# The last transform stage of one batch inside the loop, and loads asked for in another order, in a spectral layer with a gated feed-forward on one core

## Chip, cores and metric

The kernel runs on one core of a Trainium2 chip. The metric is the device time of one execution in microseconds (us). Before the change its median is 1721.03 us over three runs (1718.88 to 1724.48).

## What is computed

```python
X = np.fft.rfft(x, axis=1)                      # x: 8 batches x 3136 x 256
Yr = Xr @ w_r - Xi @ w_i + b_r
Yi = Xr @ w_i + Xi @ w_r + b_i
Yr = np.sign(Yr) * np.maximum(np.abs(Yr) - 0.01, 0.0)     # and Yi alike
y = np.fft.irfft(Y, n=3136, axis=1)
h = np.maximum(y @ w_in, 0.0)                   # 256 -> 1024
conv_out = sum(conv_w[k] * hp[:, k:k + S, :] for k in range(3))
out = (h * (1.0 / (1.0 + np.exp(-conv_out)))) @ w_out     # 1024 -> 256
```

The three feed-forward weights come as float64 and are turned into pairs of float32 values (a high and a low part) on the chip.

## The kernel before

The program has two halves. The first, the transform loop, does the Fourier transform, the complex weights, the shrinking and the first half of the inverse transform. The second, the feed-forward loop, finishes the inverse transform (stage 4) batch by batch and runs the two large matrix products.

**Transform loop.** The work is 56 items, seven per batch (`items`, line 385). An item goes through stage 1 (`stage1_pe`, `stage1_out`, line 272: load 224 KB x 2 of x, multiply, copy the result `a1` out of PSUM by ACT and DVE, store it to a scratch tensor `sc1`), stage 2 (`stage2`, line 313, which reads the scratch back as `a2`), `third` (ACT, then POOL writes `fl`), `mix` (line 341, three PSUM banks of 12 matmuls each, then DVE adds into `p1` and `v`), `shrink` (two ACT Relu into `r` and `q`, then POOL subtracts) and `stage3_pe`/`stage3_out` (line 364 and 370, result `z1` stored to the scratch `sc2`). The items are pipelined: in pass `it` of the loop PE does stage 3 of item `it-4`, stage 1 of an item some eight ahead, stage 2 of item `it` and the mix of item `it-1`. The whole half stands under `manual_schedule`, so each engine executes in the order in which the code is written. Stage 1 reads ahead by three loads of x (`fetch(XRB)`), a2 is asked for one or two passes ahead, except at a batch's first item, which is asked for one pass ahead.

**The head.** Ahead of the loop, `stage1_head` does stage 1 of batch 0's seven items. Half of each x load and all of the `ha` stores are issued by ACT, the rest by SP. Between the x loads and the first a2 load SP also asks for the first mixing weights (`load_mix`), two pieces of the table t2, and four more x loads (`fetch(2)`).

**Weights.** From pass 7 on, a generator `later()` is advanced three steps a pass (lines 432 to 439). Each step is one DVE instruction of the float64 conversion; the DMA that brings a piece (`load_bits`, line 201) is one of its steps, asked for while the piece before it is converted. The table i2 and the convolution weights `cw` are asked for after the last piece.

**Between the halves.** Stage 4 (`stage4`, lines 473 to 495) reads back 448 KB of `sc2` as `z2`, does 8 matmuls (line 482; the trace shows 16 records, as each fp32 matmul goes in two passes) into two PSUM banks, and moves them to `yh` (ACT, line 488) and `yl` (DVE, line 489), two or three strided pieces each, ACT and DVE in turn. A batch takes seven calls. Batch 0's seven stand ahead of the feed-forward loop, after the transform's last pass, since the memory for y (two tiles of 25 KB a partition) is free only then. Here, and in the whole second half, a scheduler orders the instructions.

**Feed-forward loop.** 224 steps of `up` (12 matmuls, line 507, then ReLU, the three-tap convolution, sigmoid and gating on ACT and DVE) and, four steps later, `down` (21 matmuls, line 535). Stage 4 of the next batch is put in at f = 1, 4, 7.

All DMA commands of one engine are issued in program order, and a command that waits holds those behind it. A command also waits until the one eight places before it, whose completion counter it takes over, is done.

Of the kernel before, what the change touches and what calls it, by code (L numbers as in the profile page):

```python
# [18 lines left out]
R = 56  # L19
U = 28  # L20
SL = 57
SP = 64
# [8 lines left out]
CH = 448  # L31

# [92 lines left out]
def spectral_ffn_kernel(ctx: ExitStack, tc: tile.TileContext, x, w_r, w_i, b_r, b_i,  # L125
# [18 lines left out]

    with ExitStack() as ab:
        stg = ab.enter_context(tc.tile_pool(name="stg", bufs=1))
        wbp = ab.enter_context(tc.tile_pool(name="wbp", bufs=2))
        s1p = ab.enter_context(tc.tile_pool(name="s1p", bufs=2))
# [7 lines left out]
        f1 = c1.tile([P, P], F32, name="f1")[:, 0:SP]  # L156
# [41 lines left out]
        def load_bits(src, n, name):  # L198

            raw = wbp.tile([P, n, 2], I32, name=f"{name}_bits", tag="bits")  # L200
            nc.sync.dma_start(raw.rearrange("p (a b) w -> p a b w", a=src.shape[1]) if len(src.shape) == 4 else raw, src)
            return raw
# [33 lines left out]
        def later():  # L236
# [7 lines left out]
            for n in range(len(pieces) + 1):  # L244
                if n < len(pieces):
                    dst, src, nm = pieces[n]
                    asked.append((dst, load_bits(src, WP, nm), WP, nm))
                    yield None
                if n:
                    yield from split_weight(*asked.pop(0))  # L250
            nc.sync.dma_start(i2, inv2.rearrange("p (a m) -> p a m", a=2))
            bits = [load_bits(conv_w[k].rearrange("(f p) w -> p f w", p=P), NF, "cw") for k in range(2)]
            for k in range(3):
                top, rest = yield from from_bits(bits[k], NF, "cw")
                yield nc.vector.tensor_tensor(cw[:, k, :], top, rest, op=ALU.add)
                if k == 0:
                    bits.append(load_bits(conv_w[2].rearrange("(f p) w -> p f w", p=P), NF, "cw"))

        def load_x(pool, b, jc, q=nc.sync, **kw):
# [3 lines left out]
            for h in range(2):  # L263
                (q if h else nc.sync).dma_start(xr[SP * h:SP * h + R], xv[h, :, jc * JC:(jc + 1) * JC, :])
# [9 lines left out]
        def store_a1(b, jc, a1, q=nc.sync):  # L274
            dst = sc1[b].rearrange("m (c r j) d -> r c m (j d)", r=2, j=4)
            for r in range(2):
                q.dma_start(dst[r, jc], a1[SP * r:SP * r + R].rearrange("p j h d -> p (j h d)"))  # L277
# [14 lines left out]

        def stage1_head(xs):

            with tc.tile_pool(name="ha", bufs=1, reuse_waits="tile") as ha:
                for jc, xr in enumerate(xs):
                    a1 = ha.tile([P, 2, 2, D], F32, name=f"ha{jc}")
                    copy_a1(a1, stage1_pe(xr))
                    store_a1(0, jc, a1, nc.scalar)
# [28 lines left out]
        def mix(xs):  # L328
# [13 lines left out]
            p1 = wk.tile([K2, 2, UG // 2, D], F32, name="p1")  # L342
            v = wk.tile([K2, 2, UG // 2, D], F32, name="v")
            for c in range(2):
                nc.vector.tensor_tensor(p1[:, c], ps[2], bias[:, c:c + 1, :].to_broadcast([K2, UG // 2, D]), op=ALU.add)
            for c in range(2):
                nc.vector.tensor_tensor(v[:, c], ps[c], p1[:, c], op=ALU.add)
            return v

        def shrink(v):  # L350
            r = wk.tile([K2, 2, UG // 2, D], F32, name="r", bufs=3)
            q = wk.tile([K2, 2, UG // 2, D], F32, name="q", bufs=1)
            nc.scalar.activation(r, v, AF.Relu, bias=mlam)
            nc.scalar.activation(q, v, AF.Relu, bias=mlam, scale=-1.0)  # L354
            nc.gpsimd.tensor_tensor(r, r, q, op=ALU.subtract)  # L355
# [43 lines left out]
        with tc.tile_pool(name="hx", bufs=1, reuse_waits="tile") as hx:  # L399
            xh = [load_x(hx, 0, p, nc.scalar, tag=f"hx{p}") for p in range(NG)]  # L400
            load_t2(0)
            raw = load_mix()
            fetch(2)
            load_t2(1)
            stage1_head(xh)
            split_mix(raw)
            a2s = {i: load_a2(*items[i]) for i in range(2)}
# [7 lines left out]
        background = later()  # L415
        for it in range(n_it + LAG):
# [15 lines left out]
            if WP0 <= it < n_it:  # L432
                next(background, None)
# [166 lines left out]
```

## Time and profile before

| | |
|---|---|
| median of three runs | 1721.03 us |
| the profiled execution's own time | 1719.61 us |
| its span in the trace | 1717.8 us, so 1.8 us lie around it |
| PE busy | 1676.3 us |
| DVE, ACT, POOL busy | 1390.6, 1197.7, 209.9 us |
| granted PE clock over the span | 0.989 |
| mean share of the DMA engines busy in the first 430 us | 0.7 to 0.9 and over |

Rows of the view of waits read: engine, tile and line that waited, what ended the wait, total us, times, longest. Rows of the chain and of the timeline read: start, duration, engine, line, operation, tile written and read; in the timeline the bracket gives the engine's idle time just before it and what ended it. Rows of the windows give the stretch, then each engine's busy us with its count, the granted PE clock, the mean share of the 16 DMA engines, GB/s. Consecutive PE records overlap by some tenths of a us, so prices are taken from start to start.

### The profile page before, as it was taken

To read this page: it belongs to the slowest core of one execution; us is meant where nothing else is said; L and a number is where in the kernel's file an instruction comes from. 1 tells how busy PE (TensorE), PEld (TensorE's weight loads), DVE (VectorE), ACT (ScalarE), POOL (GpSimd) and SP (SyncE) were. 2 spreads that over 40 slices of the span, in tenths; PEclk is the share of its full clock that TensorE was granted. 3 is DMA by queue.
4 is the path that set the end of the run, shared out by engine and by line. 5 is a ranking of instruction groups with operands and counts; after the bars stand their busy time and mean duration, and the time that the engine had idled before them with its cause. 6 is when DMAs were issued, how large, how long until landed. Compare 5 with 4: busy or idle time off the path is not lost.

```text
span 1717.8 us, 30462 instructions
## 1 busy us (share of the span) xinstructions
PE 1676.3 (98%) x12544; PEld 1553.5 (90%) x12544; DVE 1390.6 (81%) x1722; ACT 1197.7 (70%) x1589; POOL 209.9 (12%) x116
## 2 busy tenths in 40 slices
PE   4999999999989999999999999999999999999998
PEld 1888888888878999999999999999999999999998
DVE  2678888776547888888888888888888888888887
ACT  2667777767656777777777777777777777777676
POOL 0344544444520000000000000000000000000000
PEclk7999999999999999999999999999999999999999
DMA  8998888788441110111111011111101111100001
GB/s 242 265 268 256 238 248 246 222 233 219 122 126 34 55 43 22 54 55 33 54 45 43 22 55 52 35 55 44 43 22 55 48 39 47 40 22 23 22 22 44
DMA packets 109002, 163.77 MB, mean 95 GB/s; under 512 B 10680, under 2 KB 87728, under 8 KB 108864
## 3 DMA queue, kind: packets, MB, share of 16 engines
q1 hardware_dynamic: 107394, 157.01, 31.4%
q10 hardware_dynamic: 1470, 4.82, 0.8%
q8 instruction: 99, 1.62, 0.4%
q14 instruction: 39, 0.32, 0.1%
HBM read 84.73 MB, written 77.07 MB: 94 GB/s over the span
## 4 chain that ended last, share of the span: by engine, by line
PE 96%; DMA 2%; ACT 1%; DVE 1%; issue 0%; ACTq 0%; POOL 0%; SPq 0%
PE acc L535 32%; PE ps_h L507 32%; PE ps_mx L341 14%; PE ps_s L313 7%; PE ps_s L482 6%; PE ps_s L364 3%; PE ps_s L272 3%; DMA xr<-in_x_dram 1%; DMA sc<-ha 0%; DVE yl L489 0%; DMA sc<-a 0%; ACTq L277 0%; DMA sc<-z 0%; DVE c L516 0%; ACT yh L488 0%
## 5 line engine op out<-in xcount | busy, mean ns | idle before, releaser
L535 PE MATMUL acc<-wout,gh 128*128 128x256 f32 x3136 | 571.2, 281 | 0.0
L516 DVE SCALAR_TENSOR_TENSOR c<-h,cw,c 128x896 f32<-128x896 f32 x448 | 512.0, 1146 | 69.7 <-ACT c L514 66.7
L507 PE MATMUL ps_h<-yh,win 128*128 128x450 f32 x1792 | 550.1, 368 | 3.0 <-ACT yh L488 2.0
L535 PEld LDWEIGHTS acc<-wout,gh 128*128 128x128 f32 x3136 | 493.0, 188 | 6.1 <-ACT gh L521 0.2
L535 PE MATMUL acc<-wout,gl 128*128 128x256 f32 x1568 | 437.3, 280 | 0.4 <-DVE gl L522 0.4
L507 PEld LDWEIGHTS ps_h<-yh,win 128*128 128x128 f32 x1792 | 339.5, 189 | 29.3 <-ACT yh L488 2.2
L509 ACT ACTIVATE h<-ps_h 128x900 f32<-128x900 f32 x224 | 207.0, 924 | 197.8 <-PE ps_h L507 197.4
L507 PE MATMUL ps_h<-yl,win 128*128 128x450 f32 x896 | 329.9, 368 | 0.2 <-DVE yl L489 0.2
L535 PEld LDWEIGHTS acc<-wout,gl 128*128 128x128 f32 x1568 | 293.8, 188 | 1.2 <-DVE gl L522 0.6
L518 DVE TENSOR_TENSOR c<-h,c 128x896 f32<-128x896 f32 x224 | 243.2, 1086 | 40.9 <-ACT c L517 40.1
L522 DVE TENSOR_TENSOR gl<-c,gh 128x896 fp32r<-128x896 f32 x224 | 242.5, 1088 | 41.7 <-ACT gh L521 40.8
L521 ACT CAST gh<-c 128x896 fp32r<-128x896 f32 x224 | 210.7, 941 | 85.7 <-DVE c L518 85.7
L517 ACT ACTIVATE c<-c 128x896 f32<-128x896 f32 x224 | 212.4, 948 | 20.3 <-DVE c L516 18.3
L341 PE MATMUL ps_mx<-wmix_hi,fh 128*128 128x256 f32 x672 | 192.6, 287 | 0.0
L341 PE MATMUL ps_mx<-wmix_hi,fl 128*128 128x256 f32 x672 | 188.3, 280 | 1.7 <-POOL fl L325 1.7
L341 PE MATMUL ps_mx<-wmix_lo,fh 128*128 128x256 f32 x672 | 187.5, 279 | 0.0
L507 PEld LDWEIGHTS ps_h<-yl,win 128*128 128x128 f32 x896 | 169.5, 189 | 11.6 <-DVE yl L489 0.5
L514 ACT ACTIVATE c<-h,cw 128x896 f32<-128x896 f32 x168 | 176.0, 1047 | 1.8
L355 POOL TENSOR_TENSOR r<-r,q 128x1024 f32<-128x1024 f32 x56 | 133.4, 2382 | 236.8 <-ACT q L354 229.3
L313 PEld LDWEIGHTS ps_s<-t,a 112*128 112x128 f32 x896 | 106.0, 194 | 54.4 <-issue 47.9
L341 PEld LDWEIGHTS ps_mx<-wmix_hi,fl 128*128 128x128 f32 x672 | 126.3, 188 | 2.5 <-POOL fl L325 1.9
L313 PE MATMUL ps_s<-t,a 112*128 112x128 f32 x896 | 117.0, 284 | 10.9 <-issue 10.2
(75 smaller groups left out, 1713.3 us busy)
## 6 DMA issues: line engine op xcount, KB each, us to landing
a<-sc SPq DMA_DIRECT2D x56, 448.0 KB
z<-sc SPq DMA_DIRECT2D x56, 448.0 KB
out_dram<-o SPq DMA_DIRECT2D x27, 896.0 KB
xr<-in_x_dram SPq DMA_DIRECT2D x105, 224.0 KB
sc<-z SPq DMA_DIRECT2D x104, 224.0 KB
sc<-a SPq DMA_DIRECT2D x98, 224.0 KB
sc<-ha ACTq DMA_DIRECT2D x14, 224.0 KB
win_bits<-in_moe_w_in_dram SPq DMA_DIRECT2D x4, 512.0 KB
```

Source lines behind the costliest of these rows:

```text
L313: nc.tensor.matmul(ps[:, k], a2[:, k, t * P:(t + 1) * P], t2[:, g * UG + k, :], start=(k == 0), stop=(k == UG - 1), skip_group_check=True)
L341: nc.tensor.matmul(ps[c][:, k, :], lt, rh, start=(n == 0), stop=(n == len(mm) - 1))
L355: nc.gpsimd.tensor_tensor(r, r, q, op=ALU.subtract)
L507: nc.tensor.matmul(ps[:, a, 0:CH + 2], lt, rh, start=(n == 0), stop=(n == len(mm) - 1))
L509: nc.scalar.activation(h, ps[:, :, 0:CH + 2], AF.Relu)
L514: nc.scalar.mul(c, h[:, :, 0:CH], cw[:, 0, f:f + 1])
L516: nc.vector.scalar_tensor_tensor(c, h[:, :, k:k + CH], cw[:, k, f:f + 1], c, op0=ALU.mult, op1=ALU.add)
L517: nc.scalar.activation(c, c, AF.Sigmoid)
L518: nc.vector.tensor_tensor(c, h[:, :, 1:CH + 1], c, op=ALU.mult)
L521: nc.scalar.copy(gh, c)
L522: nc.vector.tensor_tensor(gl, c, gh.bitcast(F32), op=ALU.subtract)
L535: nc.tensor.matmul(acc[m // 2][:, m % 2, :], lt[:, sl], rh[:, f, :], start=(f == 0 and n == 0 and m % 2 == 0), stop=(f == NF - 1 and n == ...
```

## The change

Four things are changed.

1. Stage 4 of batch 0 moves into the transform loop: one call in each of the passes 48 to 52 and one in 57 and 58. The memory of the conversion, of x and of a1 is given back in pass 47 and taken by `z2` and `y`; p1 and q are dropped (DVE adds into `v` in place, ACT's second Relu writes `v` in place). In the loop a call works on two single banks, one after the other; the seven moves of batch 0 are so made in halves.
2. In the head, SP issues everything; four x loads are ahead, and each further one stands behind a store. `load_mix` comes after the fourth store, the first t2 piece after the sixth; only two of the four further x loads stand ahead of the first a2.
3. The first weight piece, i2 and all three cw pieces are asked for in pass 5; each further piece one conversion earlier than it is worked on.
4. Moves of one stage-4 call are regrouped: ACT's pieces first, then DVE's. In the feed-forward loop, the call at step 1 is left out (`st > 1`), so batch 1's first call is at step 4.

```diff
+    def stage4(jg, z2, y, banks):
+        for ts, ps in banks():
...
+            for src, (hi, lo) in parts:
+                nc.scalar.copy(hi, src)
+            for src, (hi, lo) in parts:
+                nc.vector.tensor_tensor(lo, src, hi.bitcast(F32), op=ALU.subtract)
...
+            nc.sync.dma_start(i2, inv2.rearrange("p (a m) -> p a m", a=2))
+            bits = [load_bits(conv_w[k].rearrange("(f p) w -> p f w", p=P), NF, "cw", bufs=1, tag=f"cw{k}") for k in range(3)]
+            ask(0)
+            yield None
+            for n in range(len(pieces)):
+                if n + 1 < len(pieces):
+                    ask(n + 1)
+                yield from split_weight(*asked.pop(0))
...
-            p1 = wk.tile([K2, 2, UG // 2, D], F32, name="p1")
             v = wk.tile([K2, 2, UG // 2, D], F32, name="v")
             for c in range(2):
-                nc.vector.tensor_tensor(p1[:, c], ps[2], bias[:, c:c + 1, :].to_broadcast([K2, UG // 2, D]), op=ALU.add)
+                nc.vector.tensor_tensor(v[:, c], ps[2], bias[:, c:c + 1, :].to_broadcast([K2, UG // 2, D]), op=ALU.add)
...
-            nc.scalar.activation(q, v, AF.Relu, bias=mlam, scale=-1.0)
-            nc.gpsimd.tensor_tensor(r, r, q, op=ALU.subtract)
+            nc.scalar.activation(v, v, AF.Relu, bias=mlam, scale=-1.0)
+            nc.gpsimd.tensor_tensor(r, r, v, op=ALU.subtract)
...
+            for _ in range(4):
+                ask_x()
+            for jc in range(NG):
+                a1 = ha.tile([P, 2, 2, D], F32, name=f"ha{jc}")
+                copy_a1(a1, stage1_pe(xh[jc]))
+                store_a1(0, jc, a1)
+                ask_x()
+                if jc == 3:
+                    raw = load_mix()
+                if jc == 5:
+                    load_t2(0)
+            split_mix(raw)
+            load_t2(1)
+            fetch(1)
+            a2s = {i: load_a2(*items[i]) for i in range(2)}
             fetch(2)
...
-            if WP0 <= it < n_it:
+            if WP0 <= it < Y0:
                 next(background, None)
+            elif it == WP0 - 2:
+                next(background)
...
+            if it == Y0:
+                eb.close()
+                zio, y_a = pool("zio", 3, side="right"), pool("y_a", side="right")
+                y0 = new_y(y_a)
+                z2s = []
+                for _ in range(3):
+                    ask_z2()
...
+            if Y0 < it < Y1 or n_it < it <= n_it + 2:
+                jg, z2 = z2s.pop(0)
+                stage4(jg, z2, y0, one_by_one)
+                ask_z2()
...
-    ys = {0: new_y(0)}
-    for jg in range(NPC):
-        with tc.high_priority(offset=HP):
-            stage4(0, jg, ys[0])
+    ys = {0: y0}
...
-            if todo and f in (1, 4, 7):
+            if todo and f in (1, 4, 7) and st > 1:
```

The order of the instructions, at three places. First SP in the head, from its first command to the first a2 load (`a_246`, after the change `a_249`); `sc_0` is the scratch of batch 0, `ha` the head's results, `t` the table t2, `wm_raw` the mixing weights. Before:

```order
L264 DMA xr<-in_x_dram 56x1024 x7
L173 DMA t_108<-in_fwd_dram 112x512
L179 DMA wm_raw_144<-in_w_r_dram 128x2x256
L179 DMA wm_raw_145<-in_w_i_dram 128x2x256
L264 DMA xr<-in_x_dram 56x1024 x4
L173 DMA t_108<-in_fwd_dram 112x512
L303 DMA a_246<-sc_0_57 112x4x256
```

And now:

```order
L308 DMA xr<-in_x_dram 56x1024 x2
L321 DMA sc_0_57<-ha_186 56x1024 x2
L222 DMA wm_raw_197<-in_w_r_dram 128x2x256
L222 DMA wm_raw_198<-in_w_i_dram 128x2x256
L321 DMA sc_0_57<-ha_201 56x1024 x2
L321 DMA sc_0_57<-ha_212 56x1024 x2
L216 DMA t_115<-in_fwd_dram 112x512
L321 DMA sc_0_57<-ha_224 56x1024 x2
L216 DMA t_115<-in_fwd_dram 112x512
L308 DMA xr<-in_x_dram 56x1024 x2
L339 DMA a_249<-sc_0_57 112x4x256
```

SP now carries the 14 stores as well, each waiting for a copy of ACT and DVE with the next loads behind it, and four x loads and one t2 piece that stood ahead of the last store no longer do.

Second, SP in passes 5 and 6, from pass 5's `z` stores to the a2 loads of items 7 and 8 (`sc_1` is the scratch of batch 1, `i_76` is i2). Before:

```order
L373 DMA sc_0_65<-z_715 56x1024
L379 DMA sc_0_65<-z_715 56x1024
L277 DMA sc_1_58<-a_719 56x1024 x2
L264 DMA xr<-in_x_dram 56x1024 x2
L196 DMA i_266<-in_inv_dram 128x256
L303 DMA a_801<-sc_1_58 112x4x256
L303 DMA a_803<-sc_1_58 112x4x256
```

And now:

```order
L407 DMA sc_0_65<-z_715 56x1024
L413 DMA sc_0_65<-z_715 56x1024
L291 DMA i_76<-in_inv_dram 112x224
L244 DMA cw_bits<-in_moe_conv_w_dram 128x8x2 x3
L244 DMA win_bits<-in_moe_w_in_dram 128x1024
L321 DMA sc_1_58<-a_728 56x1024 x2
L308 DMA xr<-in_x_dram 56x1024 x2
L239 DMA i_273<-in_inv_dram 128x256
L339 DMA a_808<-sc_1_58 112x4x256
L339 DMA a_810<-sc_1_58 112x4x256
```

Five loads now stand ahead of the last a1 store of batch 1, whose landing the a2 load of item 7 waits for.

Third, PE between the last mix (`ps_mx`) and the first matmul of the feed-forward loop (`ps_h`). Before, the end of that stretch, the last two of the three stage 3 (`r,i`), the call between them and the first of the four behind them (a call's two rows come twice and are shown once):

```order
L364 MATMUL ps_s_6057<-r,i_266 64x256 x8
L482 MATMUL ps_s_6162<-i_76,z_6160 128x2x56 x3
L482 MATMUL ps_s_6162<-i_76,z_6160 128x112
L364 MATMUL ps_s_6070<-r,i_266 64x256 x8
L482 MATMUL ps_s_6177<-i_76,z_6175 128x2x56 x3
L482 MATMUL ps_s_6177<-i_76,z_6175 128x112
```

And now, the whole stretch from the last mix on:

```order
L398 MATMUL ps_s_6059<-r,i_273 64x256 x8
L171 MATMUL ps_s_6076<-i_76,z_5486 128x2x56 x3
L171 MATMUL ps_s_6076<-i_76,z_5486 128x112
L171 MATMUL ps_s_6085<-i_76,z_5486 128x2x56 x3
L171 MATMUL ps_s_6085<-i_76,z_5486 128x112
L398 MATMUL ps_s_6094<-r,i_273 64x256 x8
L171 MATMUL ps_s_6107<-i_76,z_5592 128x2x56 x3
L171 MATMUL ps_s_6107<-i_76,z_5592 128x112
L171 MATMUL ps_s_6116<-i_76,z_5592 128x2x56 x3
L171 MATMUL ps_s_6116<-i_76,z_5592 128x112
L398 MATMUL ps_s_6125<-r,i_273 64x256 x8
L542 MATMUL ps_h<-yh,win_78 128x450
```

Two of the seven calls are left here, between the last three stage 3, and the feed-forward loop follows the last stage 3 at once.

More of the change, by code (lines that the diff above doesn't have):

```diff
@@ L31 @@
 CH = 448
+SW = 3168
 def _tables():
@@ new lines, in load_z2, with part @@
+    def load_z2(b, jg, zio):
+        z2 = zio.tile([K1, JG, D], F32, name="z2")
+        nc.sync.dma_start(z2, sc2[b].rearrange("j q u e -> (q u) j e")[:, jg * JG:(jg + 1) * JG, :])
+        return z2
+    def stage4(jg, z2, y, banks):
+        for ts, ps in banks():
+            psv = ps[:, :, 0:JG * K1].rearrange("p t (w m) -> p t w m", m=R)
+            for n, t in enumerate(ts):
+                for j in range(JG):
+                    to = psv[:, n, j:2 * JG - j:2 * JG - 1 - 2 * j, :]
+                    nc.tensor.matmul(to, z2[:, j, t * P:(t + 1) * P], i2[:, 0 if jg or j else 1, :], start=(j == 0), stop=(j == JG - 1),
+                                     skip_group_check=True)
+            def part(w0, n, r0):
+                return psv[:, :, w0:w0 + n, :].rearrange("p t j m -> p t m j"), [
+                    q[:, ts[0]:ts[-1] + 1, 1:S + 1].rearrange("p t (m r) -> p t m r", r=R)[:, :, :, r0:r0 + n] for q in y]
+            r1 = R - jg * JG - JG + 1
+            parts = [part(0, JG, jg * JG)] + ([part(JG, JG, r1)] if jg else [part(JG, JG - 1, r1), part(2 * JG - 1, 1, H)])
+            for src, (hi, lo) in parts:
+                nc.scalar.copy(hi, src)
+            for src, (hi, lo) in parts:
+                nc.vector.tensor_tensor(lo, src, hi.bitcast(F32), op=ALU.subtract)
@@ L243, in later, with ask @@
             asked = []
[L244 to L250, printed above, removed]
-            nc.sync.dma_start(i2, inv2.rearrange("p (a m) -> p a m", a=2))
-            bits = [load_bits(conv_w[k].rearrange("(f p) w -> p f w", p=P), NF, "cw") for k in range(2)]
+            def ask(n):
+                dst, src, nm = pieces[n]
+                asked.append((dst, load_bits(src, WP, nm), WP, nm))
+            nc.sync.dma_start(i2, inv2.rearrange("p (a m) -> p a m", a=2))
+            bits = [load_bits(conv_w[k].rearrange("(f p) w -> p f w", p=P), NF, "cw", bufs=1, tag=f"cw{k}") for k in range(3)]
[5 more added lines that the diff above has]
+                yield from split_weight(*asked.pop(0))
             for k in range(3):
@@ L291, in stage1_out @@
             store_a1(b, jc, a1)
[L293 to L299, printed above, removed]
         def load_a2(b, g):
@@ L398, in spectral_ffn_kernel, with ask_x @@
         load_f1()
[L399 to L402, printed above, removed]
+        with tc.tile_pool(name="hx", bufs=1, reuse_waits="tile") as hx, tc.tile_pool(name="ha", bufs=1, reuse_waits="tile") as ha:
+            xh = []
+            def ask_x():
+                if len(xh) < NG:
+                    xh.append(load_x(hx, 0, len(xh), tag=f"hx{len(xh)}"))
+            for _ in range(4):
[13 more added lines that the diff above has]
+            a2s = {i: load_a2(*items[i]) for i in range(2)}
             fetch(2)
[L404 to L407, printed above, removed]
             load_bias()
@@ L415, in spectral_ffn_kernel, with one_by_one, ask_z2 @@
         background = later()
+        Y0, Y1 = n_it - NPC - 2, n_it - 3
+        jgs = iter(range(NPC))
+        def one_by_one():
+            for t in range(NT):
+                yield range(t, t + 1), psx.tile([P, 1, 512], F32, name="ps_s4", tag="bank")
+        def ask_z2():
+            jg = next(jgs, None)
+            if jg is not None:
+                z2s.append((jg, load_z2(0, jg, zio)))
         for it in range(n_it + LAG):
@@ L436, in spectral_ffn_kernel @@
                 p1 += 1
-            if WP0 <= it < n_it:
+            if WP0 <= it < Y0:
                 for _ in range(2):
```

80 lines of the change are left out of this document (29 added, 51 removed).

## The prediction

> **What bounds the kernel now.** First the page: PE is busy nearly throughout, so only what PE loses can be won.
>
> ```profile
> PE 1676.3 (98%) x12544; PEld 1553.5 (90%) x12544; DVE 1390.6 (81%) x1722; ACT 1197.7 (70%) x1589; POOL 209.9 (12%) x116
> ```
>
> Of 1717.8 us of span 41.5 us are PE idle. The matmuls stay the same in number and shape, so the sum is made of PE's waits and of stretches at a low clock. The view of PE's waits names them:
>
> ```profile
> PE ps_s L313 <- issue: 10.2, 1, 10.2
> PE ps_s L272 <- ACT ha L280: 7.9, 2, 4.2
> PE ps_s L482 <- DVE yl L470: 3.2, 1, 3.2
> PE ps_h L507 <- ACT yh L488: 2.0, 1, 2.0
> PE ps_mx L341 <- POOL fl L325: 1.7, 1, 1.7
> PE ps_s L272 <- issue: 1.5, 2, 0.9
> PE ps_s L482 <- DVE yl L489: 1.5, 1, 1.5
> PE ps_h L507 <- ACT h L509: 1.0, 1, 1.0
> ```
>
> Lines 272 and 313 are the head and the transform loop, 341 the loop's last mix, 482 and 507 the seam between the two halves. The change aims at three places; each is costed by itself.
>
> **The head.** PE's first stage 2 starts when the first a2 has come back from the scratch. The timelines of SP, ACT and PE show what sets that:
>
> ```profile
> 14.39 1.89 ACTq L277 DMA_DIRECT2D sc<-ha  x2
> 28.76 1.01 ACTq L277 DMA_DIRECT2D sc<-ha  x2
> 32.45 0.87 SPq L303 DMA_DIRECT2D a<-sc  x2
> 36.53 3.75 PE L313 MATMUL ps_s<-t,a 112*128 112x128 f32 x16 [10.18 <-issue]
> 15.00:20.00 5.00, 2.08 (x8) 0.40 (x8) 0.69 (x1) 0.58 (x1) 0.00 (x0) 0.58 0.96 248
> 25.00:30.00 5.00, 1.35 (x8) 0.00 (x0) 1.30 (x2) 1.94 (x4) 0.00 (x0) 0.84 0.89 360
> ```
>
> The first store leaves ACT only at 14.39, the last at 29.77, lands by 32.45, and the a2 load takes 4.1 us more. The DMA engines are 89 to 96% busy (last column but one of the windows): the head is a matter of bytes and of their order. Ahead of the last store the change takes away four x loads of 224 KB and one t2 piece of 224 KB, 1.15 MB; at the 248 GB/s of the load stretch that is 4.6 us. One t2 piece and two x loads (0.69 MB, 2.8 us) come back between the last store and the first a2; the 2.7 us from the last store's issue to the a2's (29.77 to 32.45) hide most of that, but the tail of the queue delays the a2 by about 0.5 us. SP's new order costs something too: 21 commands more (7 half loads, 14 stores), a store holding the next x load until ACT and DVE have copied. Four x loads (1.8 MB, 7 us of transfer) lie ahead, longer than load, matmul and copy of one; so the transfers stay fed, and I take 1.1 us for it. Sum: 4.6 - 0.5 - 1.1 = 3.0 us gained. Bounds: 4.6 gained if all is hidden; 1.1 lost if the single file leaves the engines empty once for the 4.1 us of a round trip.
>
> The Trainium skill (DMA: Bandwidth & Descriptors, section Issuing engines are not separate DMA queues) says that issuing from several engines saves only the issuing time, since all run on the same 16 engines. By it alone the move of commands from ACT to SP would give nothing and the gain would be the 4.1 us of bytes and order; the trace says a little more, as ACT's copies here stand behind its own blocked stores (the store at 14.39).
>
> **Weights.** A pass of the loop takes 8.08 us from mix to mix (85.80 to 93.88 in the chain); two passes take longer, and DVE's timeline shows why:
>
> ```profile
> 85.80 4.21 PE ps_mx L341 x36
> 93.88 4.21 PE ps_mx L341 x36
> 104.13 1.87 PE ps_mx L341 x16
> 99.37 0.43 DVE L213 TENSOR_SCALAR win_e<-win_bits 128x512 int32<-128x512 int32 x1 [6.70 <-DMA win_bits<-in_moe_w_in_dram]
> 330.17 4.21 PE ps_mx L341 x36
> 340.19 1.87 PE ps_mx L341 x16
> 334.53 1.09 DVE L213 TENSOR_SCALAR cw_e<-cw_bits 128x8 int32<-128x8 int32 x1 [5.56 <-DMA cw_bits<-in_moe_conv_w_dram]
> ```
>
> DVE executes in order. It reached a conversion step before its load had landed, and the moves of stages 1 and 2 waited behind it until PE ran out of PSUM banks (the "issue" waits of line 272). Price: 104.13 - 93.88 - 8.08 = 2.17 us and 340.19 - 330.17 - 8.08 = 1.94 us. Now the first piece and cw are asked for in pass 5 and used from pass 7 on, 16 us later: both waits go, 4.1 us. Their DVE work is the same; the cw ones now run ahead of pass 44. At least the idle part, 1.5 us, must come back.
>
> But five loads in pass 5 now stand on SP ahead of the last a1 store of batch 1, and item 7's a2 waits for that store:
>
> ```profile
> 77.98 1.31 SPq L277 DMA_DIRECT2D sc<-a  x2
> 83.67 0.86 SPq L303 DMA_DIRECT2D a<-sc  x2
> 91.89 1.98 PE ps_s L313 x16
> 331.34 1.62 SPq L201 DMA_DIRECT2D cw_bits<-in_moe_conv_w_dram  x2
> ```
>
> Before, store 77.98, a2 issued 83.67, landed at about 87.8 (4.1 us as above), needed at 91.89: 4.1 us to spare. The five loads hold the store: 512 KB at 248 GB/s are 2.1 us, i2 0.4, three cw about 1.0 each (two were asked for from 331.34 and DVE went on at 334.53, 3.2 us later with the fixed part of a transfer), 5.5 us. That is 1.4 us of stall; the head, shorter by 3 us and with 0.46 MB of x pushed behind it, leaves the DMA engines less time, which may add as much again in part. I take 2.0 us lost, between 0 and 6.
>
> The Trainium skill (DMA: Bandwidth & Descriptors, Specifications) names 512 B as the least transfer for full rate; cw goes in 8-byte pieces, so the rule speaks against putting it into the fullest stretch. The row above, two of them within 3.2 us, bounds the harm; the rule's price is not stated there, and if it is larger, the first rival below holds.
>
> **The seam.** PE's timeline and chain, with POOL and ACT:
>
> ```profile
> 492.15 3.83 PE L482 MATMUL ps_s<-i,z 112*128 112x112 f32 x32
> 495.90 1.09 PE L364 MATMUL ps_s<-r,i 64*64 64x256 f32 x16
> 495.46 2.38 POOL L355 TENSOR_TENSOR r<-r,q 128x1024 f32<-128x1024 f32 x1 [4.99 <-ACT q L354]
> 508.55 6.44 PE L482 MATMUL ps_s<-i,z 112*128 112x112 f32 x32 [3.25 <-DVE yl L470]
> 516.97 0.47 PE L507 MATMUL ps_h<-yh,win 128*128 128x450 f32 x1 [1.99 <-ACT yh L488]
> 517.63 6.48 PE ps_h L507 x23
> 536.04 2.46 PE ps_h L507 x12
> 508.00:516.00 8.00, 6.44 (x32) 6.29 (x32) 3.20 (x7) 2.38 (x4) 0.00 (x0) 0.62 0.55 145
> L488 ACT CAST yh<-ps_s 128x448 fp32r<-128x448 f32 x104 | 63.5, 613 | 40.5 <-PE ps_s L482 21.5 <-DVE yl L489 18.2 <-DVE yh L470 0.7
> L488 ACT CAST yh<-ps_s 128x112 fp32r<-128x112 f32 x8 | 3.0, 370 | 0.0
> ```
>
> A stage-4 call is 16 records: 495.90 - 492.15 = 3.75 for two, 1.88 us each at full clock. From 492.15 to the feed-forward's first matmul at 516.97 pass 24.8 us: seven calls (13.1), two stage 3 (2.1), three waits (1.5 + 3.2 + 2.0) and 2.6 us of low clock (6.44 - 3.83; granted 0.62 in that window). Now five calls stand in passes 48 to 52, 9.4 us of PE work that does not vanish, and PE is full there. Behind the last mix are two stage 3 and two calls, 5.9 us. The last stage 3 waits for POOL, 495.46 + 2.38 = 497.84, where PE arrives at 497.0: 0.9 us idle, over at 499.0. The feed-forward needs the last call's moves: ACT is free of `r` and `v` at 495.5, then come four half moves, the `z` copy of 1024 columns, four half moves. A half move of 224 columns lies between 0.37 and 0.61, 0.45 by the slope, 0.4 from start to start; the `z` copy 1.0 by the same slope: 8 x 0.4 + 1.0 = 4.2, the last ends at 499.7, DVE's last at about 500.3, the first half of the columns 0.8 us earlier. So the first matmul comes near 499.8, plus the 9.4 us moved ahead: 509.2 against 516.97, 7.8 us gained.
>
> PE then arrives without a gap above 2 us, so the feed-forward should begin at full clock: 23 matmuls took 6.48 where 12 take 2.46, so 6.48 - 4.72 = 1.8 us gained. Of the 1.0 us wait of line 507 on ACT I let half go, 0.5 us, since no stage-4 move stands between the first steps on ACT. Seam: 7.8 + 1.8 + 0.5 = 10.1 us gained; bounds 6 (DVE again held behind the memset of the next y, 3.2, and no clock gain) and 13.
>
> What covers the moved calls, and where a pass without stage 1 has its bound:
>
> ```profile
> 471.99 4.39 PE ps_mx L341 x36
> 479.39 4.40 PE ps_mx L341 x36
> 450.00:480.00 30.00, 30.00 (x275) 26.92 (x276) 17.37 (x33) 21.25 (x34) 14.38 (x8) 1.00 0.34 95
> 427.61 0.37 ACT L316 COPY d<-ps_s 128x256 f32<-128x256 f32 x1 [0.39 <-POOL fl L325]
> ```
>
> Such a pass lasts 7.4 us; ACT is busy 21.25 / 30 x 7.4 = 5.2 of it, DVE 4.3. With a call it lasts 9.3 on PE, ACT needs 5.2 + 4 x 0.45 = 7.0, DVE 6.1: covered. The three z2 loads in pass 47 stand ahead of item 49's a2 on SP, 1.3 MB or 5.5 us, when the loads of x have ended, and that a2 is used over 15 us later. The memset of y in pass 47 waits on DVE for the last a1 store, with the mix adds behind it; DVE has 3 us to spare. Without cover each would cost up to 5 us.
>
> The other edits cost nothing: regrouped moves and the call left out at step 1 (four steps to spare at batch 1's first use) lie under a PE that is never idle in the feed-forward loop; `v` in place adds a wait of ACT on itself, under 0.2 us a pass. The loop ACT, POOL, ACT over the single buffer `d` (the last row above) sets the 7.4 us of passes without stage 1; passes with it take 8.08, so 0.68 is to spare.
>
> **Sum.** 1719.6 - 3.0 - 4.1 + 2.0 - 10.1 = 1704.4 for the profiled run, which lies 1.4 below the median; so 1705.8.
>
> **Rivals.**
> 1. DMA becomes the bound of passes 2 to 9: stalls of 6 us and a head that gives 1. For it: the x loads pushed behind the head, cw's small pieces. Against it: three x loads of lead, and before the change the waits of lines 272 and 313 behind the head add up to little beyond the two of the weights. 1719.6 - 1 - 4.1 + 6 - 10.1 = 1710.4, as a median 1711.8. Chance 0.17.
> 2. The seam keeps a stall: DVE held by the next y's memset until the last `z` store lands, or last moves late; seam 6 instead of 10.1: 1709.9. Chance 0.14.
> 3. Slower: the loop over `d` and `v` grows. ACT's in-place Relu must wait for the first, POOL's subtract for it, ACT's next `d` for POOL. It decides from 0.68 us a pass on; at 1.2 us, PE loses 0.52 in some 45 passes, 23 us: 1705.8 + 23 = 1729. Against it: one wait of an engine on itself was never that dear here (DVE's `v` already followed its own `p1`). Chance 0.04.
> 4. The change does not do what it says: the moved calls block PE in pass 48, since z2 must wait for freed memory. Five us, 1710.8. Chance 0.05.
>
> Forecast 0.60. About 0.3% (5.2 us) is what a measurement of this kernel can tell from no change. Faster by more: forecast, rivals 1, 2 and 4 nearly whole, 0.91; within: 0.06; slower: 0.03. The range reaches over rivals 1, 2 and 4: 1701 to 1713.
>
> **What would show it.** Right: first stage 2 near 33.5; no DVE wait on win_bits or cw_bits; mix rows 8.08 apart up to pass 47 but for one gap near pass 7, and 9.1 to 9.3 apart in passes 48 to 52; first ps_h matmul some 5 us behind the last mix plus stage 4's two calls, at clock 1.00. Wrong: mix rows over 8.1 apart throughout (rival 3), repeated waits of line 272 or 313 on DMA in passes 2 to 9 (rival 1), a wait of over 2 us at the first ps_h matmul (rival 2).

## The result, and the profile after

The changed kernel takes 1702.97 us in the median of four runs (1701.72 to 1706.47); the kernel before, in four runs on the same chip, 1722.76 us (1718.88 to 1727.06). The ratio is 0.9888 with a 95% interval of 0.9858 to 0.9917: some 19 us faster, between 14 and 24 by the interval. The profiled execution of the changed kernel is the slowest of its four: 1706.47 us, span 1704.7 us. The forecast was 1705.8 us in a range of 1701 to 1713.

The page of the kernel after: PE's busy time is the same within 1.3 us, so the gain is idle time and clock.

```profile
PE 1677.6 (98%) x12544; PEld 1554.2 (91%) x12544; DVE 1400.5 (82%) x1737; ACT 1203.2 (71%) x1604; POOL 209.9 (12%) x116
```

1704.7 - 1677.6 = 27.1 us of PE idle time, against 41.5 before. PE's waits in the kernel after:

```profile
PE ps_s L349 <- DMA a<-sc: 13.4, 2, 10.5
...
PE ps_mx L377 <- POOL fl L361: 1.8, 1, 1.8
```

Of the waits of before, ACT's copies in the head (7.9), both waits of line 482 (3.2 and 1.5), the 2.0 at the first `ps_h` and both waits behind weight conversions are gone. In the head PE now waits for the x loads instead of ACT; what ends that stretch is the a2 load. Line 349 (stage 2) waits for a2 twice: 10.5 us in the head and 13.4 - 10.5 = 2.9 us once more. The chain of the kernel after shows where that second wait stands, and what the whole transform loop does:

```profile
28.10 5.79 DMA a<-sc
33.98 3.75 PE ps_s L349 x16
...
66.92 4.20 PE ps_mx L377 x36
81.16 6.51 DMA sc<-a
87.75 4.21 DMA a<-sc
92.09 3.75 PE ps_s L349 x16
95.85 5.18 PE ps_mx L377 x36
104.90 4.20 PE ps_mx L377 x36
...
419.50 4.20 PE ps_mx L377 x36
428.48 4.25 PE ps_mx L377 x36
...
493.77 5.79 PE ps_mx L377 x34
507.55 12.53 PE ps_h L542 x60
```

Read it from the top. The last store of the head now ends in time for an a2 load at 28.10, and the first stage 2 starts at 33.98 instead of 36.53: 2.55 us won. Then, in pass 7, the store of batch 1's last a1 (81.16) and the a2 load behind it (87.75) are on the chain: the stall that the prediction had priced at 2.0. At 104.90 the kernel after is 0.8 us behind the kernel before (104.13 at the same mix): in this execution pass 7 ate the head's gain and the 2.17 us of the weight wait together. From there the mixes come 8.07 us apart with no gap at the convolution weights, where the kernel before lost 1.94 us; they come 9.0 apart in passes with a call of stage 4, and the first `ps_h` follows the last mix by 13.8 us, against 30.0 before.

The balance of the two profiled executions, from these rows and those of before: the mix of pass 47 stands at 419.50 instead of 420.91 (1.4 won), from there to the first `ps_h` 88.05 instead of 96.06 (8.0 won), from there to the end 1197.15 instead of 1200.83 (3.7 won). Together 13.1, the difference of the spans.

SP in the kernel after, ahead of that a1 store, shows what holds it:

```profile
75.94 0.67 SPq L291 DMA_DIRECT2D i<-in_inv_dram  x1
76.66 3.36 SPq L244 DMA_DIRECT2D cw_bits<-in_moe_conv_w_dram  x3
80.07 0.58 SPq L244 DMA_DIRECT2D win_bits<-in_moe_w_in_dram  x1
80.75 0.79 SPq L321 DMA_DIRECT2D sc<-a  x2
```

Three cw loads take SP 3.36 us to issue, 1.1 us each; the 512 KB weight piece takes 0.58. The windows of the kernel after show what came behind the two waits of pass 7 and of the last mix:

```profile
90.00:95.00 5.00, 2.91 (x14) 2.94 (x14) 0.78 (x2) 0.77 (x2) 0.07 (x1) 0.61 1.00 315
...
494.00:500.00 6.00, 6.00 (x46) 5.74 (x50) 2.39 (x4) 0.80 (x1) 2.37 (x1) 0.73 0.17 55
```

The granted clock (third number from the end) is 0.61 behind the first, 0.73 behind the second. The stage 2 at 92.09 took 3.75 us instead of 2.05, the mixes 5.18 and 5.79 instead of 4.2.

### The profile page after: what moved, and what is told of

Same layout as the page of the kernel before. It is cut to its first block, busy times and chain, and to the rows that moved or that the text cites. A ratio compares the mean times of both kernels' runs of the same rounds, so it can differ in the third digit from the quotient of the medians.

```text
span 1704.7 us, 30596 instructions
## 1 busy us (share of the span) xinstructions
PE 1677.6 (98%) x12544; PEld 1554.2 (91%) x12544; DVE 1400.5 (82%) x1737; ACT 1203.2 (71%) x1604; POOL 209.9 (12%) x116
## 4 chain that ended last, share of the span: by engine, by line
PE 96%; DMA 2%; ACT 1%; SPq 1%; issue 0%; DVE 0%; POOL 0%; ACTq 0%; DVEq 0%; POOLq 0%
PE ps_h L542 32%; PE acc L570 32%; PE ps_mx L377 13%; PE ps_s L349 7%; PE ps_s L171 6%; PE ps_s L398 3%; PE ps_s L316 3%; DMA a<-sc 1%; DMA xr<-in_x_dram 1%; DMA sc<-a 0%; DMA wm_raw<-in_w_i_dram 0%; SPq L244 0%; DMA sc<-ha 0%; ACT yh L180 0%; SPq L308 0%
## 5 line engine op out<-in xcount | busy, mean ns | idle before, releaser
L552 ACT ACTIVATE c<-c 128x896 f32<-128x896 f32 x224 | 213.2, 952 | 27.1 <-DVE c L551 23.5
L389 POOL TENSOR_TENSOR r<-r,v 128x1024 f32<-128x1024 f32 x56 | 133.5, 2384 | 253.1 <-ACT v L388 245.3
L349 PE MATMUL ps_s<-t,a 112*128 112x128 f32 x896 | 118.3, 287 | 14.3 <-DMA a<-sc 13.4
```

Source lines behind the costliest of these rows:

```text
L349: nc.tensor.matmul(ps[:, k], a2[:, k, t * P:(t + 1) * P], t2[:, g * UG + k, :], start=(k == 0), stop=(k == UG - 1), skip_group_check=True)
L389: nc.gpsimd.tensor_tensor(r, r, v, op=ALU.subtract)
L552: nc.scalar.activation(c, c, AF.Sigmoid)
```

## Experiments

The theory on record had three parts: a head that gains by order and bytes, two weight waits that go at the price of a new stall in pass 7, and a seam that carries most of the gain. The first three runs take one part each. Every time is the median of four or more executions, and every ratio is to executions of the kernel before on the same chip, but for one run that is named. Line numbers shift from run to run with the edits.

**The new head alone** (kernel before, stage 1 of batch 0 in the order of the kernel after):

```diff
-            xh = [load_x(hx, 0, p, nc.scalar, tag=f"hx{p}") for p in range(NG)]
-            load_t2(0)
-            raw = load_mix()
...
+            for _ in range(4):
+                ask_x()
+            for jc in range(NG):
...
+                store_a1(0, jc, a1)
+                ask_x()
...
-            load_t2(1)
-            stage1_head(xh)
```

> The kernel before with the new head alone. Theory (the head is bytes and order): the first stage 2 starts near 34.0 us, as it does after the whole change, 2.5 us earlier than before, and the time falls by 2.5 us. Rival (DMA is the bound of the passes behind the head): the first stage 2 is as early, but PE waits on loads in passes 1 to 9 and the time falls by 0 to 0.5 us.

Median 1720.17 us, ratio 0.9983 (0.9968 to 0.9998): 1.6 us won, with 0.3 to 5.5 inside the interval, so that the time alone does not decide between theory and rival. The first stage 2 starts at 33.64, and behind it PE waits for a load once (1.5 us for t2 in pass 2). The chain of this kernel, and where its DVE waits for the first weight piece:

```profile
90.80 4.21 PE ps_mx L333 x36
103.12 4.20 PE ps_mx L333 x36
```

```profile
96.97 0.43 DVE L213 TENSOR_SCALAR win_e<-win_bits 128x512 int32<-128x512 int32 x1 [7.37 <-DMA win_bits<-in_moe_w_in_dram]
```

The mix of pass 7 stands at 90.80, 3.1 us ahead of before (93.88). The next one stands at 103.12, only 1.0 ahead (104.13): two thirds of the gain are given back in this execution at the wait that the other part takes away. The piece lands 2.4 us earlier than before (DVE goes on at 96.97 instead of 99.37), so the wait itself takes back 0.7. The other 1.4 are the stage 2 behind it, 3.61 us in the chain instead of 2.22, at a granted clock of 0.54 from 99.4 to 103.1 us.

**The new weight requests alone** (kernel before, loads asked for as after):

```diff
-            for n in range(len(pieces) + 1):
-                if n < len(pieces):
...
+            bits = [load_bits(conv_w[k].rearrange("(f p) w -> p f w", p=P), NF, "cw", bufs=1, tag=f"cw{k}") for k in range(3)]
+            ask(0)
...
+            elif it == WP0 - 2:
+                next(background)
```

> The kernel before with the new requests for weights alone. Theory (five loads ahead of the a1 store delay item 7's a2 whatever the head is): both DVE waits go, 4.1 us, but the a2 of item 7 is issued near 89.7 instead of 83.67, lands near 93.9 and PE waits 2 us in pass 7, with up to 2.7 us of low clock behind it: the time falls by 0 to 2 us. Rival (the stall comes only because the shorter head leaves DMA too little time): no wait in pass 7, the time falls by 4 us.

Median 1718.98 us, ratio 0.998 (0.997 to 0.999): 2.8 us won (1.7 to 5.2 by the interval), more than the 0 to 2 that were expected. PE's waits in this kernel:

```profile
PE ps_s L314 <- DMA a<-sc: 3.0, 1, 3.0
```

The stall of pass 7 is there with the old head too, 3.0 us long; the shorter head does not make it. No gap at cw; from pass 8 on the mixes come 8.07 apart. The mix of pass 7 itself took 5.39 us instead of 4.2, at a granted clock of 0.66 from 95 to 100 us: low clock behind the wait here too.

**The seam alone** (kernel after with the old head and the old requests):

```diff
-            ask(0)
-            yield None
...
+        def stage1_head(xs):
...
-            elif it == WP0 - 2:
-                next(background)
```

> The changed kernel with the old head and the old requests for weights, so the seam alone. Theory: the feed-forward starts 8 us earlier than before and wins 2 to 3 us more behind that (clock and first waits): the time falls by 10 to 11 us. Rival (the seam gave what the head and the weights are credited with, or less): it falls by 15 us or more, or by 6 or less.

Median 1710.47 us, ratio 0.9929 (0.9909 to 0.9949): 11.3 us won (9 to 16 by the interval). The first `ps_h` came without a wait. In the trace the mix of pass 47 stands at 422.81, and from there to the end of the span pass 1285.2 us, against 1296.9 before: 11.7 won. The three parts alone add to 1.6 + 2.8 + 11.3 = 15.7 us, some 4 less than the whole. What the head gives back when it stands alone may be a part of that (2.1 us in its trace); the rest is within the three intervals.

**The kernel after once more:**

> The changed kernel unchanged, for a second profile on another execution. Theory (the wait of pass 7 is set by the order on SP and by the transfers): PE waits 2 to 4 us on a2 in pass 7 again and the time is 1702 to 1704 us, some 19 us below the kernel before. Rival (the wait of pass 7 belonged to that one execution): no wait in pass 7, and a time 4 to 5 us below the profiled 1706.5 us.

Median 1701.74 us, ratio 0.9874 (0.9859 to 0.989); the profiled execution has a span of 1698.2 us, 6.5 less than the first one. The windows of this execution of the same program:

```profile
90.00:95.00 5.00, 5.00 (x44) 5.00 (x45) 2.93 (x6) 3.84 (x7) 0.00 (x0) 1.00 0.96 311
...
494.00:500.00 6.00, 5.10 (x53) 4.24 (x50) 1.28 (x5) 5.71 (x11) 2.36 (x1) 1.00 0.54 151
```

The waits are nearly the same: line 349 waits 13.0 us for a2 (10.7 in the head, so 2.3 in pass 7), the last mix 1.9 for POOL. But here no low clock follows either of them. And the chain:

```profile
65.38 4.20 PE ps_mx L377 x36
...
100.00 4.20 PE ps_mx L377 x36
...
414.60 4.20 PE ps_mx L377 x36
...
488.87 4.24 PE ps_mx L377 x34
501.09 12.53 PE ps_h L542 x60
```

Against the rows of the first execution: 1.5 us are won by 65.38 (there 66.92), 3.4 more by the mix of pass 8 (34.62 us on, there 37.98), 1.6 more from the last mix to `ps_h` (12.2, there 13.8). Of the 3.4 the shorter wait is 0.6; the other 2.7 are the slow stage 2 (3.75 - 2.05) and mix (5.18 - 4.20) quoted above. So a wait of 2 to 3 us costs itself, and in some executions 1.6 to 2.7 us more for the clock behind it.

**What makes the stall of pass 7: the cw loads later, the weight piece left where it was.**

```diff
-            nc.sync.dma_start(i2, inv2.rearrange("p (a m) -> p a m", a=2))
-            bits = [load_bits(conv_w[k].rearrange("(f p) w -> p f w", p=P), NF, "cw", bufs=1, tag=f"cw{k}") for k in range(3)]
...
             for n in range(len(pieces)):
+                if n == 2:
+                    nc.sync.dma_start(i2, inv2.rearrange("p (a m) -> p a m", a=2))
+                    bits = [load_bits(conv_w[k].rearrange("(f p) w -> p f w", p=P), NF, "cw", bufs=1, tag=f"cw{k}") for k in range(3)]
```

> The kernel after, with i2 and the three cw loads asked for later (a few passes on, in the stretch of the conversion's third piece) and only the first weight piece left in pass 5 ahead of batch 1's last a1 store. My theory: the wait of stage 2 in pass 7 (2.3 to 3.0 us in the kernel after) comes from the store standing behind 3.4 us of SP's time for the three cw loads. Without them the store leaves some 3.4 us earlier and the wait ends near 0, at most 1 us; the time falls by 2 to 5 us against the kernel after (the 5 where low clock followed the wait), to 1697 to 1700 us. Rival: the wait comes from the 512 KB piece and from DMA engines that are full there; then 2 us or more of the wait stay, and the time stays within 1 us of the kernel after (1702 us). No wait of DVE on cw_bits under either.

Median 1699.19 us, ratio 0.9874 (0.9858 to 0.989). SP in this kernel:

```profile
74.26 0.70 SPq L244 DMA_DIRECT2D win_bits<-in_moe_w_in_dram  x1
75.07 1.29 SPq L322 DMA_DIRECT2D sc<-a  x2
```

The store leaves at 75.07 instead of 80.75, that is 1.65 us behind the first of the two `z` stores ahead of it (73.42) instead of 5.64 (75.11). The wait is gone (line 350 waits for a2 once, in the head) and the mixes run 8.07 apart through pass 7 (90.20 and 98.27). The 512 KB piece is still ahead of the store, and the DMA engines are about as full (0.95 from 40 to 80 us and 0.90 from 80 to 100, against 0.97 and 0.85 in the kernel after), so the rival falls: the stall came from SP's time to issue three loads in 8-byte pieces and i2, 4.0 us.

From the store to the a2 load that waits for it pass 6.8 us here, 7.0 and 5.3 in the two executions of the kernel after, 5.2 with the requests alone. So in these traces the store was no slower behind the cw loads than without them, but its own time varies by nearly 2 us, and the length of the wait in pass 7 hangs on that too. In time the gain is not shown: the medians fell by 2.5 to 3.8 us, but the ratio to the kernel before is 0.9874 here and 0.9888 and 0.9874 for the kernel after, with intervals that overlap.

**No new load ahead of the store at all** (the kernel above, and the first piece in pass 6):

```diff
-            elif it == WP0 - 2:
+            elif it == WP0 - 1:
```

> The kernel of the run before this one, with the first weight piece asked for one pass later as well (pass 6), so that no new load stands ahead of batch 1's last a1 store. My theory: no wait of stage 2 in pass 7 at all, pass 8's mix 8.1 us behind pass 7's, and the piece, asked for some 8 us ahead of its first use, lands in time; 1697 to 1700 us. Rival (full DMA engines, whatever the order): a wait of 1 us or more stays at stage 2 in pass 7, or DVE waits over 1 us for win_bits, and nothing is gained over the kernel with only cw moved.

Median 1699.81 us, ratio 0.9877 (0.986 to 0.9895). No wait in pass 7, as in the run above, so the piece itself cost nothing there. But DVE in this kernel comes to the conversion before the piece has landed:

```profile
89.61 0.43 DVE L256 TENSOR_SCALAR win_e<-win_bits 128x512 int32<-128x512 int32 x1 [2.26 <-DMA win_bits<-in_moe_w_in_dram]
```

A wait of 2.26 us on DVE, against 6.70 in the kernel before, and it does not reach PE: the mixes stay 8.07 apart (90.49, 98.56). The expectation that the piece would be in time failed: a wait of over 1 us on DVE and nothing gained over the run above are what the rival named. Its ground, a stall of stage 2 by full DMA engines, is not there; DVE's slack covers the wait.

**All seven calls behind the last mix** (kernel after, memory still given back in pass 47):

```diff
-            if Y0 < it < Y1 or n_it < it <= n_it + 2:
+            for _ in range({n_it + 1: 2, n_it + 2: 2, n_it + 3: 3}.get(it, 0)):
```

> The kernel after, with all seven stage-4 calls of batch 0 behind the last mix (two, two and three, around the three last stage 3) in place of five in passes 48 to 52. The memory is still given back in pass 47, y cleared and z2 loaded there. My theory: the seam's gain is the waits that went (calls that no longer wait for memory, for z2 and for DVE's memset), not the place of the matmuls, since PE does the same 9.4 us at either place; the passes 48 to 52 fall to about 7.3 us each, the calls reappear behind the last mix at 1.9 to 2.6 us each, and the time is 0 to 3 us above the kernel after: 1702 to 1705 us. Rival: work inside the loop hides the moves and loads, and at the end it does not; each call then waits for z2 (three buffers, about 4 us a load) or for its moves, and 5 to 9 us of the seam's 11 are lost: 1707 to 1711 us.

Median 1708.23 us (1704.89 to 1711.57), ratio 0.9924 (0.9903 to 0.9944): some 6 us more than the kernel after, twice what my theory allowed. PE's last two calls in this kernel, and the first `ps_h`:

```profile
501.45 3.79 PE L171 MATMUL ps_s<-i,z 112*128 112x112 f32 x32 [1.75 <-DMA z<-sc]
505.08 0.47 PE L542 MATMUL ps_h<-yh,win 128*128 128x450 f32 x1
```

and the chain's rows around it:

```profile
414.70 4.20 PE ps_mx L377 x36
...
482.14 4.27 PE ps_mx L377 x34
```

Against the second execution of the kernel after: the stretch from the mix of pass 47 to the last mix shrinks from 74.27 us to 67.44, by 6.8, not by the 9.4 us that the theory put for five calls; the stretch from the last mix to `ps_h` grows from 12.2 to 22.9, by 10.7: five calls (9.0 to 9.4) and two waits for z2, 2.3 us together, less the 0.9 us that the last stage 3 no longer waits. Together 3.9; the span is 4.9 longer, and the other executions of this kernel are 3 to 7 us above its profiled one, which no trace here explains. So both theories were half right. The rival's waits are real (the z2 loads can no longer hide), and the calls inside the loop cost it less than PE's own time for them: without them the eight passes from 48 to the last mix come 7.5 us apart (60.24 us), while in the kernel after the passes behind the calls come 7.2 apart. In pass 7, where SP's order is that of the kernel after, the mixes stand at 82.67 and 92.03: a wait of 1.25 us, which the view puts down to DVE, with no low clock behind it.

**One call ahead of the last mix** (the kernel with all new loads behind the store):

```diff
-            if Y0 < it < Y1 or n_it < it <= n_it + 2:
+            if Y0 < it < Y1 - 1 or n_it <= it <= n_it + 2:
```

> The kernel with no new load ahead of batch 1's last a1 store, and one stage-4 call of batch 0 taken out of pass 52 and put into pass 56, ahead of the last mix. My theory: the last mix waited 1.84 us for POOL while PE had nothing else; the call (1.88 us) fills that, the mix then follows without a gap and at full clock, so 1.8 us go for sure and 1.6 us of low clock where that followed: 1695 to 1698 us. Rival: the moves of the call keep ACT or DVE from the last items' third, POOL comes later by as much, and the wait stays at 1 us or more: no gain over the kernel without this move.

Median 1697.73 us (1696.4 to 1701.67), ratio 0.9867 (0.9847 to 0.9886), the fastest of all by median, though its interval overlaps those of the two kernels it is built from. The chain:

```profile
485.91 4.23 PE ps_mx L378 x34
498.14 12.53 PE ps_h L543 x60
```

The wait of the last mix on POOL is gone from PE's waits, and `ps_h` starts 2.0 us earlier than in the kernel without this move (500.18), 0.1 of which was there at pass 46 already (404.98 against 405.09). So the trace shows the 1.9 us; the granted clock behind the wait was full in that kernel's profile, so nothing more was to be won there in that execution.

**The first a2 loads ahead of t2 and x** (the kernel above):

```diff
             split_mix(raw)
+            a2s = {i: load_a2(*items[i]) for i in range(2)}
             load_t2(1)
-            fetch(1)
-            a2s = {i: load_a2(*items[i]) for i in range(2)}
             fetch(2)
```

> The kernel with later loads and one call moved ahead of the last mix (median 1697.7 us), and in the head the first two a2 loads ahead of the second t2 piece and of all four further x loads (0.69 MB). In the kernel after the a2 landed 5.8 us after its issue, against 4.1 us before; the prediction had put 0.5 us on that tail. My theory: the tail is worth 1.5 to 2.5 us, so the first stage 2 starts near 31 to 32 in place of 33.4, the matmuls behind it follow without a gap above 1 us, and the time falls by 1 to 2.5 us, to 1695 to 1697 us. Rival: the DMA engines are the bound of the whole stretch up to pass 9; the x and t2 loads asked for later then come too late, waits of line 317 or 350 on DMA behind the first stage 2 add up to 1.5 us or more, and the time is the same within 1 us or longer.

Median 1699.64 us, ratio 0.9878 (0.9859 to 0.9896): nothing gained, nor clearly lost, against 1697.73. The chain, and after it that of the kernel it is built from:

```profile
27.60 4.18 DMA a<-sc
31.87 3.75 PE ps_s L350 x16
35.62 5.50 PE ps_s L317 x16
41.13 3.63 PE ps_s L350 x16
44.75 4.24 PE ps_mx L378 x36
52.00 4.24 PE ps_mx L378 x36
```

```profile
27.97 5.39 DMA a<-sc
...
49.95 4.24 PE ps_mx L378 x36
```

The tail was worth what the theory said: a2 lands in 4.18 us instead of 5.39, and stage 2 starts 1.6 us earlier (33.44 in the other kernel). The matmuls behind it then ran slowly for longer: two items of stage 1 took 5.50 us instead of 3.12, the second stage 2 3.63 instead of 2.05, and the mix of pass 2 came at 52.00 instead of 49.95, 2.05 us later. The rival's waits on DMA did not appear. None of the other three executions (1699.52 to 1701.36) was faster than the profiled one (1699.06), which speaks for the order rather than for this execution; no trace of another execution decides it, and it stays open.

**v in place, alone** (kernel before; a single execution, no median):

```diff
-            p1 = wk.tile([K2, 2, UG // 2, D], F32, name="p1")
...
-                nc.vector.tensor_tensor(v[:, c], ps[c], p1[:, c], op=ALU.add)
+                nc.vector.tensor_tensor(v[:, c], ps[c], v[:, c], op=ALU.add)
...
-            nc.scalar.activation(q, v, AF.Relu, bias=mlam, scale=-1.0)
-            nc.gpsimd.tensor_tensor(r, r, q, op=ALU.subtract)
+            nc.scalar.activation(v, v, AF.Relu, bias=mlam, scale=-1.0)
+            nc.gpsimd.tensor_tensor(r, r, v, op=ALU.subtract)
```

> The kernel before, with nothing changed but v: DVE adds into v in place and ACT's second Relu writes v in place, p1 and q dropped. Calls stay behind the loop. My theory, from the kernel with all calls at the end, where ACT's two Relu start 1.22 us apart instead of 1.05 and the last passes come 7.57 us apart instead of 7.40: ACT waits for itself, the loop ACT, POOL, ACT grows by 0.15 to 0.2 us and the passes 49 to 55 of this kernel come 7.55 to 7.6 us apart; passes with stage 1 stay at 8.07 to 8.08. The time grows by about 1.2 us at most (1720 to 1723 us in one look). Rival: the longer passes there come from the z2 loads and the clearing of y; then this kernel's last passes stay at 7.40 to 7.42 us.

ACT in this kernel, in a pass without stage 1:

```profile
447.61 0.38 ACT L316 COPY d<-ps_s 128x256 f32<-128x256 f32 x1 [1.21 <-POOL fl L325]
...
449.09 1.19 ACT L351 ACTIVATE r<-v,small 128x1024 f32<-128x1024 f32 x1
450.31 1.16 ACT L352 ACTIVATE v<-v,small 128x1024 f32<-128x1024 f32 x1
...
455.18 0.37 ACT L316 COPY d<-ps_s 128x256 f32<-128x256 f32 x1 [1.22 <-POOL fl L325]
```

The two Relu start 1.22 us apart (1.05 before: 451.37 and 452.42), and the pass lasts 455.18 - 447.61 = 7.57 us instead of 7.43. Passes with stage 1 stay at 8.07. So the in-place edit costs 0.15 us in each pass that nothing else covers (the first three passes without stage 1 still last 7.2). From the mix of pass 48 to the last one this kernel takes 60.20 us (432.84 to 493.04), the kernel before 58.84 (428.12 to 486.96), 1.4 more, a little over the 1.2 that was put. Its one time, 1724.68 us, is 5.1 above the profiled execution of before; beside these passes the wait for the first weight piece was 4.4 longer in it (the mixes around it stand at 93.58 and 108.20), which has nothing to do with the edit.

## Why the prediction was right, and where it was off

The forecast case came: every wait that was to go went, the one that was to appear appeared in the pass named, and `ps_h` starts at full clock. The median came 2.8 us below the forecast, and the gain (1 - 0.9888 of 1722.76, 19.3 us) 4 above the 15.2 that was forecast. Point by point:

- **Head, 3.0.** Measured 2.55 and 3.3 in the two profiled executions (33.98 and 33.21). Right in sum by luck, two errors that nearly cancel: the a2 load left 4.35 us earlier (28.10 for 32.45), where 4.6 less 1.1 was put; its tail cost 1.7 (5.79 for 4.1), where 0.5 was put.
- **Two weight waits, 4.1.** Both gone.
- **Stall in pass 7, 2.0.** The mechanism was right, the size near: 2.9 and 2.3 us of wait in the kernel after, 3.0 with the requests alone and 1.25 with all calls at the end. The low clock behind it, 2.7 us in the first execution, the prediction left out altogether. The cw loads were priced at 1.0 us each for their transfer and cost 1.1 each in SP's time; the 512 KB piece was priced at 2.1 and held SP for 0.6. The rule of the Trainium skill (DMA: Bandwidth & Descriptors, Specifications) that pieces below 512 B miss the full rate was weighed against this change; the run with the cw loads later shows that they were indeed the harm, by the time for which they held SP. A loss on the 16 DMA engines does not show: from the store behind them to the a2 load pass 4.8 to 7.0 us, and 6.8 without them.
- **Seam, 10.1.** Measured 11.3 alone. `ps_h` came 8.0 us earlier in the balance above, 9.6 in the second execution; 7.8 was put. Behind `ps_h` 3.7 us were won, where 1.8 + 0.5 were put. So the seam is 1.2 us (alone) to 3.2 us (9.6 + 3.7 against 10.1) of the 4 that were missed. The step that failed is "9.4 us of PE work that does not vanish, and PE is full there". The chains of before and of the second execution of the kernel after show it, from pass 50 and from pass 53 on:

```profile
442.55 4.21 PE ps_mx L341 x36
449.76 4.41 PE ps_mx L341 x36
457.18 4.38 PE ps_mx L341 x36
```

```profile
466.87 4.20 PE ps_mx L377 x36
474.08 4.20 PE ps_mx L377 x36
```

Before, PE was full in the first four passes without stage 1: they lasted 7.2 us, what PE's own work takes (stage 3 1.02, stage 2 1.98, mix 4.21 in the chain). Only the next four lasted 7.4, the figure of the prediction, by the loop of ACT and POOL. Now the passes with a call last 9.0, and the ones behind them 7.2. So a call costs 1.8 us of PE there, five of them 9.0 and not 9.4, and another 0.8 comes back where four passes fall from 7.4 to 7.2: the five calls cost 74.27 - 66.05 = 8.2 us of loop, and 6.8 over the same loop with v in place. That is 1.2 of the 1.8 us by which `ps_h` came earlier than was put. Behind `ps_h`, the wait of line 507 on ACT (1.0 us) went whole, where half was put, and 0.2 on DVE with it; the other 0.7 us there have no cause shown.
- **v in place, nothing.** It costs 0.15 us a pass, within the bound of 0.2 that was put; in the kernel after nothing of it shows, as passes with stage 1 stay at 8.07 and those with or behind a call go at PE's pace.
- **The last mix.** Not in the sum: its 1.8 us wait was in the kernel before and is in the kernel after, and the low clock behind it (1.6 us in the first execution) came in some traces and not in others.

Of the rivals, 1 (DMA the bound of passes 2 to 9) falls: no repeated wait of lines 316 or 349, only pass 7's (other kernels with the new head wait once more, at most 2.0 us for t2 in pass 2). 2 (a stall at the seam) falls: no wait at the first `ps_h`. 3 (the loop over `d` and `v`) is a real mechanism at 0.15 us, a fifth of the 0.68 from which it would decide. 4 (pass 48 blocked) falls: 9.0 us from mix to mix.

The missed 4 us can be shared out for the second execution, whose span is 19.6 us shorter than before. Its mix of pass 2 stands at 49.24 in the chain, that of before at 53.52; the mixes of pass 47 at 414.60 and 420.91, the first `ps_h` at 501.09 and 516.97.

| stretch | put | second execution |
|---|---|---|
| to the mix of pass 2 (the head) | 3.0 | 4.3 |
| to the mix of pass 47 (weight waits less the stall) | 2.1 | 2.0 |
| to the first `ps_h` | 7.8 | 9.6 |
| to the end | 2.3 | 3.7 |

In the head 3.3 us were won at the first stage 2 and 1.0 right behind it, where two items of stage 1 took 2.1 us in the chain instead of 3.3; in the first execution they took 2.9, and 2.7 us were won in all.

Low clock followed the wait of the last mix in 3 of the 10 traces that have it (a mix of 5.8 us instead of 4.2), and the wait of pass 7 in 2 of 4. What decides it was not found, so what that stall costs in the median stays open.

## What to carry to other kernels

A load put early on a queue is paid for by whatever stands behind it in that queue: count the issuing time of each command by its piece size, and look for the store that someone waits for. What is won at one wait can be lost at the next wait of the same stretch: of its 3.1 us the head alone lost 0.7 at the weight wait behind it, and 1.4 to the low clock that followed there. Work that cannot vanish is best put where another engine sets the pace of the passes, since there it costs less than its own time (8.2 us of loop for 9.0 of PE).

## What the runs showed of the hardware

- The same program, with nearly the same waits of 1.8 to 2.9 us on PE, fell to a granted clock of 0.61 and 0.73 behind them in one execution and stayed at 1.00 in another; that made 4.3 of the 6.5 us between the two.
- Behind the head's wait of 9 to 12 us the first 16 matmuls of stage 2 always took 3.6 to 3.8 us, against 2.05 later; how long the slowness lasted differed from about 3.6 us (cw loads later) to 12.9 us (a2 first, 31.87 to 44.75), with PE busy all the while. The Trainium skill (TensorE: Matmul & The Clock Gate, Part 1: The HAM clock gate) says that the clock is released after one busy window of about 3.4 us and that the count of slow matmuls varies from run to run; the stretch of 3.6 us here agrees, that of 12.9 does not: in it the second stage 2 still took 3.63 us at 41.13, 9.3 us behind the start of the first.
- The granted clock in the records cannot be trusted at the start. The first 16 matmuls of stage 2 take 3.75 us in the kernel before (from 36.53) and in the kernel after (from 33.98), but the windows give 0.50 before (36 to 40 us) and 1.00 in the kernel after:

```profile
32.00:36.00 4.00, 2.02 (x9) 2.05 (x10) 0.00 (x0) 0.00 (x0) 0.00 (x0) 1.00 1.09 229
```

- In all eight traces with the new head the last two items of stage 1 ahead of the loop take 2.6 to 3.1 us for eight matmuls; in the four with the old head they take at most 2.1, and in the loop 1.04. What slows them was not found, but it costs something. In the second execution of the kernel after they stand on the chain to the first stage 2:

```profile
19.75 2.82 PE ps_s L316 x7
```

The last x load has landed by then (19.62), and DVE's copy, the last store (23.70) and the a2 load (27.78) follow. At the rate of the loop the last item would be done some 1.8 us earlier; that is an estimate from 2.81 - 1.04, which no run tried.
